# Placing the next norm's steps of both pairs between the products of the second channel matmul

## The chip, the cores and the metric

The kernel runs on one core of one Trainium2 chip. The metric is the device time of one execution in microseconds (us), as the median of several runs. Engines are named as the profile names them: PE (TensorE, matmuls), PEld (its weight loads), DVE (VectorE), ACT (ScalarE), POOL (GpSimd), SP (SyncE, which issues most DMAs here). Each engine works through its own instructions strictly in order; an instruction can wait for semaphores of other engines and of DMAs.

## The reference, cut to what matters

Three layers run one after the other on 8 x 576 = 4608 rows of 512 columns: attention with pooled keys and values, a mixture of experts, and a channel mix with a norm before it. The change lies in the last:

```python
mu = np.mean(x, axis=-1, keepdims=True)
var = np.mean((x - mu) ** 2, axis=-1, keepdims=True)
xn = (x - mu) / np.sqrt(var + 1e-06) * g_ln
ch = np.maximum(xn @ w_ch1, 0.0) @ w_ch2      # 512 -> 2048 -> 512
return (x + ch).astype(np.float32)
```

## The kernel before, in words

The attention and the experts take the first half of the time (up to about 660 us) and are not touched. After them the channel mix goes through the 4608 rows in `NG` = 9 passes of 512 rows (g = 0 to 8). A pass is `ffn1(g)` and then `ffn2(g)`: the first and the second channel matmul.

Both matmuls are computed with seven products of blocks in place of eight (`PROD`, numbered 1 to 7), and each product in fp16 with three matmuls, high half x high half, high x low and low x high (`PASS`). A product of the second matmul is one call of `mm2(i, pr)`: 8 slices x 3 = 24 matmuls of 128x256. The index i is the pair: pair 0 holds the row tiles 4g and 4g+2, pair 1 the tiles 4g+1 and 4g+3 (a tile is 128 rows). Products 1, 6, 5 and 3 of a pair accumulate one after the other in the PSUM tile `ga[i]`, products 2, 7 and 4 in `gb[i]`. Between two products the result so far must be read out of PSUM: `ev2(g, i, pr)` does it, by an ACT copy for products 1 and 6 (L1075) and 7 (L1077), by DVE for 2 (L1079), 5 (L1082), 4 (L1085) and 3. So product 6 of pair 0 can't start before ACT's copy of product 1 of pair 0, product 7 not before L1079 of the same pair, product 5 not before the copy of product 6, product 4 not before the copy of product 7. PE takes the products of `ffn2` in this order: 1 and 2 of pair 0 and 1 of pair 1 (their last slice at the end), then (1,2), (0,6), (0,7), (1,6), (1,7), (0,5), (1,5), (0,4), (1,4), written as (pair, product). Product 3 is left over and runs inside the next `ffn1`.

Meanwhile the rows of the next pass have to be normed and transposed. `ln(g, i, q)` does this for one pair. It is a Python generator of 21 steps, each of which issues one piece:

- steps 1 to 8: the statistics of both tiles on DVE (L995 to L998, L1001, L1002), with two small POOL operations (L999);
- steps 9 to 11: three ACT operations that write the normed rows into q (L1004, L1006 twice);
- steps 12 to 15: four DVE sums and differences of blocks (`combine`, L862);
- step 16: an ACT copy that rounds seven blocks to fp16, the high half `q16[:, 0]` (L1008);
- step 17: a DVE subtraction that writes the low half `q16[:, 1]` (L1009);
- steps 18 to 21: four DMA transposes issued by SP (L1014), from `q16` into `xnT`. Taken as 28 blocks of 128 columns, the transposes carry blocks 0 to 7, 8 to 15, 16 to 23 and 24 to 27. Blocks 0 to 13 are the high half, 14 to 27 the low half, two for each of the seven inputs.

There is one `q16` and one `xnT` for both pairs; q is `q32[0]` for pair 0 and `q32[1]` for pair 1 (the traces call them q and r). Every matmul of `ffn1` reads the columns of both pairs. A product of `ffn1` (`mm1`, six matmuls) takes the high half of its input in the first two matmuls and the low half in the third. Its first three products are 1, 2 and 6: they need low blocks 14 and 15 (second transpose), 16 and 17 (third) and 24 and 25 (fourth).

What sets the order is the order in which the Python code issues instructions, for each engine on its own. `tick(n)` takes n steps from a list of generators, `chains`: pair 0 first, and pair 1 once pair 0 is through. `drain()` takes all that is left.

Of the kernel before, what the change touches and what calls it, by code (L numbers as in the profile page):

```python
# [9 lines left out]
F32 = mybir.dt.float32  # L10
# [38 lines left out]
def tile_attention_moe_ffn(ctx: ExitStack, tc: tile.TileContext, a, out):  # L49
# [71 lines left out]
    with ExitStack() as at:  # L121
# [257 lines left out]
        for i in range(NT + 3):  # L379
# [49 lines left out]
            if i < NT and b + 2 < B:  # L429
                g = f - 2 if b == 0 else f  # L430
# [30 lines left out]
    def single(name, *shape, dt=F32):  # L461
        return ctx.enter_context(tc.tile_pool(name=f"{name}_p", bufs=1)).tile([128, *shape], dt, name=name)
# [5 lines left out]
    q32 = [single("q32", 8, 256), r2[:, 0:2048].rearrange("p (b x) -> p b x", x=256)]  # L468
# [37 lines left out]
    chains = []  # L506

    def tick(n=1):
        while chains and n:
            if next(chains[0], None) is None:  # L510
                chains.pop(0)
            else:
                n -= 1
# [97 lines left out]
    m2 = ctx.enter_context(tc.tile_pool(name="m2", bufs=2))  # L611
    ps_m = ctx.enter_context(tc.tile_pool(name="ps_m", bufs=2, space=PSUM))
    with ExitStack() as rt:
# [3 lines left out]
        def sb(name, *shape, dt=F32):  # L617
            return rp.tile([128, *shape], dt, name=name)
# [11 lines left out]
        st = sb("st", 2, 128)  # L630
# [225 lines left out]
    def combine(q, rows):  # L856
        if rows:
            ops = ((4, 0, 3, ADD), (5, 1, 0, SUB), (6, 1, 4, SUB), (7, 2, 6, ADD))
        else:
            ops = ((4, 0, 1, SUB), (5, 3, 0, SUB), (6, 4, 3, SUB), (7, 2, 6, ADD))  # L860
        for o, x, y, f in ops:
            yield V.tensor_tensor(out=q[:, o], in0=q[:, x], in1=q[:, y], op=f)  # L862
# [122 lines left out]
    def ln(g, i, q):  # L985
        st_t = []
        for j in (4 * g + i, 4 * g + 2 + i):
            yt = yt_t[j]
            ti = ym.tile([128, 1], U32, tag="ti", name="ti")
            ti_t[j] = ti  # L990
            st = m2.tile([128, 6], F32, tag="bs", name="bs")
            mv = m2.tile([128, 2], F32, tag="mv", name="mv")
            rs = m2.tile([128, 2], F32, tag="rs", name="rs")
            st_t.append((yt, mv, rs))
            yield V.bn_stats(out=st, in_=yt[:, 0:DM])  # L995
            yield V.bn_aggr(out=mv, in_=st)
            V.tensor_copy(out=ti, in_=yt[:, DM:YROW])
            V.tensor_scalar(out=rs[:, 0:1], in0=mv[:, 1:2], scalar1=1e-6, scalar2=None, op0=ADD)  # L998
            yield P.tensor_tensor(out=rs[:, 0:1], in0=rs[:, 0:1], in1=mhalf, op=ALU.pow)  # L999
        for yt, mv, rs in st_t:  # L1000
            V.tensor_scalar(out=rs[:, 0:1], in0=rs[:, 0:1], scalar1=SN, scalar2=None, op0=ALU.mult)  # L1001
            yield V.tensor_scalar(out=rs[:, 1:2], in0=mv[:, 0:1], scalar1=rs[:, 0:1], scalar2=-1.0, op0=ALU.mult, op1=ALU.mult)  # L1002
        (x, _, rx), (y, _, ry) = st_t
        yield A.activation(out=q[:, 1:3], in_=x[:, 0:DM].rearrange("p (b x) -> p b x", x=256), func=AF.Identity, scale=rx[:, 0:1], bias=rx[:, 1:2])  # L1004
        for h in range(2):
            yield A.activation(out=q[:, 3 * h], in_=y[:, 256 * h:256 * h + 256], func=AF.Identity, scale=ry[:, 0:1], bias=ry[:, 1:2])  # L1006
        yield from combine(q, False)
        yield A.copy(out=q16[:, 0], in_=q[:, 1:8])  # L1008
        yield V.tensor_tensor(out=q16[:, 1], in0=q[:, 1:8], in1=q16[:, 0], op=SUB)  # L1009
        dst = xnT.rearrange("p x m c t -> p (x m c) t")  # L1010
        src = q16.rearrange("p x m c -> p (x m c)")
        for n in range(0, 28, 8):
            w = min(8, 28 - n)
            yield nc.sync.dma_start_transpose(out=dst[:, n:n + w, 128 * i:128 * i + 128], in_=src[:, 128 * n:128 * n + 128 * w])  # L1014

    def drain():
        while chains:
            tick()


    NG = NT // 4
# [22 lines left out]
    def mm2(i, pr, lo=0, hi=NP):  # L1044
        m, n = PROD[pr]
        if pr == 1 and lo == 0:
            ga[i] = ps_m.tile([128, 512], F32, tag="m", name="ga")
        if pr == 2 and lo == 0:
            gb[i] = ps_y.tile([128, 512], F32, tag="y", name="gb")
        ps = (ga if pr in (1, 6, 5, 3) else gb)[i]  # L1050
        for p in range(lo, hi):
            for x, w in PASS:
                nc.tensor.matmul(  # L1053
                    out=ps[:, 0:256], lhsT=hw[:, p, x, m, 128 * i:128 * i + 128], rhs=c2w[:, p, w, n],
                    start=(pr in (1, 2, 7) and p == 0 and x + w == 0), stop=(p == NP - 1 and x == 1), skip_group_check=True,
                )

    def out_rows(j):
        P.indirect_dma_start(  # L1059
            out=out, out_offset=bass.IndirectOffsetOnAxis(ap=ti_t.pop(j), axis=0),  # L1060
            in_=yt_t.pop(j)[:, 0:DM], in_offset=None,
        )

    def ev2(g, i, pr):
        u, t, v = us[3 * i:3 * i + 3]
        X, Y = yt_t.get(4 * g + i), yt_t.get(4 * g + 2 + i)
        lo, hi = slice(0, 256), slice(256, 512)
        a2 = ga[i][:, 0:256]
        b2 = gb[i][:, 0:256] if pr != 1 else None

        def add(row, c, src):
            V.scalar_tensor_tensor(out=row[:, c], in0=src, scalar=SC, in1=row[:, c], op0=ALU.mult, op1=ADD)  # L1072

        if pr in (1, 6):
            A.copy(out=v if pr == 1 else u, in_=a2)  # L1075
        elif pr == 7:
            A.copy(out=t, in_=b2)  # L1077
        elif pr == 2:
            V.tensor_tensor(out=v, in0=b2, in1=v, op=ADD)  # L1079
            add(X, lo, v)  # L1080
        elif pr == 5:
            V.tensor_tensor(out=t, in0=a2, in1=t, op=ADD)  # L1082
            add(Y, hi, t)
        elif pr == 4:
            V.tensor_tensor(out=u, in0=b2, in1=u, op=ADD)  # L1085
            add(Y, lo, u)
            out_rows(4 * g + 2 + i)
        elif pr == 3:
            add(X, hi, a2)
            out_rows(4 * g + i)  # L1090
# [67 lines left out]

    def ffn2(g):
        L = NP - 1  # L1160
        tick(8)
        mm2(0, 2, 0, L)
        tick(7)
        mm2(1, 1, 0, L)
        for i, pr in ((0, 1), (0, 2), (1, 1)):
            mm2(i, pr, L)
            ev2(g, i, pr)
        tick(6)
        for i, pr, n in ((1, 2, 0), (0, 6, 8), (0, 7, 7), (1, 6, 0), (1, 7, 6), (0, 5, 0), (1, 5, 0), (0, 4, 0), (1, 4, 0)):
            mm2(i, pr)  # L1170
            ev2(g, i, pr)
            tick(n)
        drain()


    def ahead(k):
# [14 lines left out]
    for k in range(NF + 2):  # L1191
# [51 lines left out]
        if k in (NF - 5, NF - 2):  # L1243
            chains.append(ln(0, int(k > NF - 5), q32[0]))
# [3 lines left out]
    drain()  # L1248
    for g in range(NG):
        ffn1(g)  # L1250
        if g + 1 < NG:
            chains.extend(ln(g + 1, i, q32[i]) for i in range(2))
        ffn2(g)
    for i in range(2):
        mm2(i, 3)
# [58 lines left out]
```

## Time and profile before

| | |
|---|---|
| median of 3 runs | 1337.65 us (1333.14 to 1343.53) |
| profiled execution | 1343.89 us, of which the span from first to last instruction is 1342.1 us |
| mean granted TensorE clock | 0.984 |
| busy share of the span | PE 95%, PEld 70%, DVE 67%, ACT 47%, POOL 23% |
| one pass of the channel mix | 74.40 us (from the start of product (0,6) at 709.64 us to the same at 784.04 us) |

The profile is of one execution. Its times are in us from the first instruction. In the timeline each row is an instruction, or a run of equal ones, with start, duration, engine, line, what it writes and reads, and in brackets how long the engine had been idle before it and who ended that.

### The profile page before, as it was taken

What the parts mean: (1) busy time and instruction counts of PE and PEld (TensorE: products, weight loads), DVE (VectorE), ACT (ScalarE), POOL (GpSimd) and SP (SyncE); (2) the same over time, 40 slices, a digit from 0 to 9 for tenths busy, and PEclk for the clock granted to TensorE, in tenths of its full rate; (3) what the DMA queues carried; (4) which work ended last, traced back from release to release, by engine and by line L of the source; (5) the groups of instructions that cost most, each with busy time, mean ns of one, the idle gap of its engine ahead of it and who ended that gap; (6) DMA issues with size and microseconds to landing.
All of it is one profiled execution on the core that took longest, in us unless ns stands there. A gap on an engine that the chain in (4) does not pass through costs nothing. (4 is left out here: it accounts for less than half of the span.)

```text
span 1342.1 us, 26386 instructions
## 1 busy us (share of the span) xinstructions
PE 1280.8 (95%) x9232; PEld 938.2 (70%) x9232; DVE 898.4 (67%) x2029; ACT 624.7 (47%) x1279; POOL 302.7 (23%) x315
## 2 busy tenths in 40 slices
PE   5999988999989999998899999999999999999996
PEld 4888854444444444443488888888888888888885
DVE  6666778545565656657595867768686868778671
ACT  4667633333544535455453635444353535444340
POOL 3455513242424243331101010101000010101001
PEclk8999989999999999998899999999999999999998
DMA  8877245999999989889963645455454645554410
GB/s 265 266 245 242 88 166 146 248 200 201 226 227 196 239 170 204 210 227 255 272 223 73 213 110 185 126 156 168 120 208 99 206 98 204 119 181 139 128 70 32
DMA packets 229101, 239.94 MB, mean 179 GB/s; under 512 B 160846, under 2 KB 179534, under 8 KB 228944
## 3 DMA queue, kind: packets, MB, share of 16 engines
q1 hardware_dynamic: 190560, 154.96, 44.5%
q10 hardware_dynamic: 29184, 53.48, 14.2%
q0 software_dynamic: 9200, 29.57, 7.2%
q8 instruction: 77, 1.26, 0.4%
q14 instruction: 80, 0.66, 0.2%
HBM read 282.61 MB, written 36.62 MB: 238 GB/s over the span
## 5 line engine op out<-in xcount | busy, mean ns | idle before, releaser
L1053 PEld LDWEIGHTS <-w 128*128 128x128 f16 x3024 | 295.8, 98 | 41.9 <-issue 7.7
L583 PE MATMUL h_ps<-w,r 128*128 128x512 f16 x936 | 217.0, 381 | 12.8 <-ACTq L961 4.5
L596 PE MATMUL y_ps<-w,hTb 128*128 128x512 f16 x936 | 219.6, 385 | 8.6 <-DMA hTb<-r 4.1
L1053 PE MATMUL ga<-c2w,w 128*128 128x256 f16 x1728 | 208.1, 273 | 6.3 <-ACT hTb L1075 6.3
L596 PEld LDWEIGHTS <-hTb 128*128 128x128 f16 x936 | 92.5, 99 | 124.2 <-issue 9.6
L583 PEld LDWEIGHTS <-r 128*128 128x128 f16 x936 | 91.8, 98 | 117.6 <-issue 17.4
L1053 PE MATMUL gb<-c2w,w 128*128 128x256 f16 x1296 | 150.3, 273 | 0.0
L1059 POOL DMA_INDIRECT out_dram<-ytb,ti x26 | 29.6, 1137 | 371.7 <-DVE ytb L1072 342.1
L1039 PEld LDWEIGHTS <-ld 128*128 128x128 f16 x1008 | 98.5, 98 | 12.9 <-issue 1.0
L1039 PEld LDWEIGHTS <-r 128*128 128x128 f16 x1008 | 98.6, 98 | 12.4 <-issue 0.6
L1039 PEld LDWEIGHTS <-w 128*128 128x128 f16 x1008 | 98.6, 98 | 12.2 <-issue 0.3
L588 DVE SCALAR_TENSOR_TENSOR r<-h_ps,r 128x512 f16<-128x512 f32 x59 | 40.5, 687 | 80.0 <-ACT r L587 39.1
L604 POOL DMA_INDIRECT y_d<-ytb,sidx x39 | 41.5, 1064 | 209.9 <-ACT r L548 136.4
L522 DVE SCALAR_TENSOR_TENSOR w<-w 128x1024 f16<-128x1024 f32 x55 | 65.5, 1232 | 23.7 <-ACT w L517 21.2
L1039 PE MATMUL fa<-xnT,ld 128*128 128x256 f16 x576 | 78.6, 273 | 0.1
L1039 PE MATMUL fa<-xnT,r 128*128 128x256 f16 x576 | 78.6, 273 | 0.1
L1039 PE MATMUL fa<-xnT,w 128*128 128x256 f16 x576 | 78.6, 273 | 0.0
L517 ACT ACTIVATE w<-w 128x1024 f16<-128x1024 f32 x56 | 55.7, 1047 | 31.4 <-ACTq L963 11.1
L587 ACT ACTIVATE r<-h_ps 128x512 f16<-128x512 f32 x59 | 35.1, 594 | 74.0 <-PE h_ps L583 44.8
L268 ACT ACTIVATE p<-s,nm 128x72 f32<-128x72 f32 x288 | 65.6, 337 | 4.2 <-DVE nm L254 4.0
L1097 ACT COPY hTb<-fa 128x256 f32<-128x256 f32 x72 | 26.8, 372 | 85.7 <-PE fa L1039 85.7
L549 DVE SCALAR_TENSOR_TENSOR r<-x_ps,r 128x512 f16<-128x512 f32 x39 | 26.9, 689 | 49.7 <-ACT r L548 47.5
(247 smaller groups left out, 2121.2 us busy)
## 6 DMA issues: line engine op xcount, KB each, us to landing
w<-in_w_dram ACTq DMA_DIRECT2D x136, 1024.0 KB
ld<-c_d SPq DMA_DIRECT2D x24, 896.0 KB
w<-c_d SPq DMA_DIRECT2D x24, 896.0 KB
r<-c_d SPq DMA_DIRECT2D x24, 896.0 KB
ld<-in_c_dram ACTq DMA_DIRECT2D x48, 256.0 KB
xrow_d<-xr SPq DMA_DIRECT2D x36, 260.5 KB
kt<-in_kT_dram SPq DMA_DIRECT2D x16, 576.0 KB
qt<-in_qT_dram SPq DMA_DIRECT2D x18, 512.0 KB
```

Source lines behind the costliest of these rows:

```text
L268: nc.scalar.activation(out=p32[:, h, :], in_=s[:, h // 4, NK * (h % 4):NK * (h % 4) + NK], func=AF.Exp, bias=nm[:, h:h + 1],)
L517: A.activation(out=hi, in_=src, func=AF.Copy, scale=SW)
L522: V.scalar_tensor_tensor(out=lo[:, 0:v], in0=src[:, 0:v], scalar=SW, in1=hi[:, 0:v], op0=ALU.mult, op1=ALU.subtract)
L549: V.scalar_tensor_tensor(out=xT[:, 1], in0=pt, scalar=SX, in1=xT[:, 0], op0=ALU.mult, op1=ALU.subtract)
L583: nc.tensor.matmul(out=ps, lhsT=xT[:, x, c], rhs=s1[:, w, c, 512 * half:512 * half + 512], start=(n == 0), stop=(n == 11))
L587: A.activation(out=hs[:, 0], in_=ps, func=AF.Relu)
L588: V.scalar_tensor_tensor(out=hs[:, 1], in0=ps, scalar=0.0, in1=hs[:, 0], op0=ALU.max, op1=ALU.subtract)
L596: nc.tensor.matmul(out=ps, lhsT=hT[:, f // 4, x, f % 4], rhs=s2[:, w, f], start=(f == 0 and x + w == 0), stop=(f == 7 and x == 1),)
L604: nc.gpsimd.indirect_dma_start(out=y_d[:, :], out_offset=bass.IndirectOffsetOnAxis(ap=sidx[:, k:k + 1], axis=0), in_=yr, in_offset=None, b ...
L1039: nc.tensor.matmul(out=ps[:, 0:256], lhsT=w[:, x, m, 128 * c:128 * c + 128], rhs=xnT[:, y, n, c], start=(pr in (1, 2, 7) and i + c == 0), ...
L1053: nc.tensor.matmul(out=ps[:, 0:256], lhsT=hw[:, p, x, m, 128 * i:128 * i + 128], rhs=c2w[:, p, w, n], start=(pr in (1, 2, 7) and p == 0 an ...
L1059: P.indirect_dma_start(out=out, out_offset=bass.IndirectOffsetOnAxis(ap=ti_t.pop(j), axis=0), in_=yt_t.pop(j)[:, 0:DM], in_offset=None,)
```

## The change

The list `chains` is no longer used by `ffn2`. It makes one generator for each pair and takes the steps of either by `step(i, n)`; `full(i, pr)` is a product and its read-out. The order of the products on PE stays, and so do all instructions: only the places of the norm's steps between the read-outs change, and both norms are under way at once. Because of that the small tiles of the statistics get four buffers in place of two. The last pass has no next norm.

```diff
@@ ln
-            st = m2.tile([128, 6], F32, tag="bs", name="bs")
-            mv = m2.tile([128, 2], F32, tag="mv", name="mv")
-            rs = m2.tile([128, 2], F32, tag="rs", name="rs")
+            st = m2.tile([128, 6], F32, tag="bs", name="bs", bufs=4)
+            mv = m2.tile([128, 2], F32, tag="mv", name="mv", bufs=4)
+            rs = m2.tile([128, 2], F32, tag="rs", name="rs", bufs=4)
@@ ffn2
         L = NP - 1
-        tick(8)
+        norm = [ln(g + 1, i, q32[i]) if g + 1 < NG else iter(()) for i in range(2)]
+
+        def step(i, n):
+            for _ in range(n):
+                next(norm[i], None)
+
+        def full(i, pr):
+            mm2(i, pr)
+            ev2(g, i, pr)
+
+        step(0, 8)
         mm2(0, 2, 0, L)
-        tick(7)
         mm2(1, 1, 0, L)
         for i, pr in ((0, 1), (0, 2), (1, 1)):
             mm2(i, pr, L)
             ev2(g, i, pr)
-        tick(6)
-        for i, pr, n in ((1, 2, 0), (0, 6, 8), (0, 7, 7), (1, 6, 0), (1, 7, 6), (0, 5, 0), (1, 5, 0), (0, 4, 0), (1, 4, 0)):
-            mm2(i, pr)
-            ev2(g, i, pr)
-            tick(n)
-        drain()
+        step(0, 3)
+        step(1, 8)
+        full(1, 2)
+        step(0, 5)
+        full(0, 6)
+        step(0, 5)
+        step(1, 3)
+        full(0, 7)
+        step(1, 4)
+        full(1, 6)
+        step(1, 1)
+        full(1, 7)
+        step(1, 5)
+        for i, pr in ((0, 5), (1, 5), (0, 4), (1, 4)):
+            full(i, pr)
@@ the passes
         ffn1(g)
-        if g + 1 < NG:
-            chains.extend(ln(g + 1, i, q32[i]) for i in range(2))
         ffn2(g)
```

On ACT, in one pass, from the end of `ffn1` to the end of `ffn2`, before (q_2208 and r_2200 are q of pair 0 and of pair 1, q_2212 is `q16`, hTb holds the buffers that the copies from PSUM write):

```order
L1004 ACTIVATE q_2208<-hTb,rs 128x512
L1006 ACTIVATE q_2208<-ytb,rs 128x256 x2
L1075 COPY hTb<-ga 128x256 x2
L1008 CAST q_2212<-q_2208 128x1792
L1075 COPY hTb<-ga 128x256
L1077 COPY hTb<-gb 128x256
L1004 ACTIVATE r_2200<-hTb,rs 128x512
L1006 ACTIVATE r_2200<-ytb,rs 128x256 x2
L1075 COPY hTb<-ga 128x256
L1077 COPY hTb<-gb 128x256
L1008 CAST q_2212<-r_2200 128x1792
```

And the same stretch of ACT with the change:

```order
L1075 COPY hTb<-ga 128x256 x2
L1004 ACTIVATE q_2208<-hTb,rs 128x512
L1006 ACTIVATE q_2208<-ytb,rs 128x256 x2
L1008 CAST q_2212<-q_2208 128x1792
L1075 COPY hTb<-ga 128x256
L1004 ACTIVATE r_2200<-hTb,rs 128x512
L1006 ACTIVATE r_2200<-ytb,rs 128x256 x2
L1077 COPY hTb<-gb 128x256
L1075 COPY hTb<-ga 128x256
L1008 CAST q_2212<-r_2200 128x1792
L1077 COPY hTb<-gb 128x256
```

The copies of product 1 of both pairs now stand ahead of pair 0's norm; pair 1's norm stands ahead of the copies of (0,7) and (1,6), and pair 1's L1008 ahead of the copy of (1,7).

On DVE, behind the statistics of pair 0 (their last row stands first), before:

```order
L1002 TENSOR_SCALAR rs<-mv,rs 128x1
L862 TENSOR_TENSOR q_2208<-q_2208 128x256 x4
L1079 TENSOR_TENSOR hTb<-gb,hTb 128x256
L1072 SCALAR_TENSOR_TENSOR ytb<-hTb,ytb 128x256
L1009 TENSOR_TENSOR q_2212<-q_2208,q_2212 128x1792
L1079 TENSOR_TENSOR hTb<-gb,hTb 128x256
L1072 SCALAR_TENSOR_TENSOR ytb<-hTb,ytb 128x256
L995 BN_STATS bs<-hTb 128x6
```

With the change the twelve rows of pair 1's statistics follow on the first read-out (L1079, L1072) at once, and after their last row DVE goes on with:

```order
L1002 TENSOR_SCALAR rs<-mv,rs 128x1
L1079 TENSOR_TENSOR hTb<-gb,hTb 128x256
L1072 SCALAR_TENSOR_TENSOR ytb<-hTb,ytb 128x256
L862 TENSOR_TENSOR q_2208<-q_2208 128x256 x4
L1009 TENSOR_TENSOR q_2212<-q_2208,q_2212 128x1792
L862 TENSOR_TENSOR r_2200<-r_2200 128x256 x4
L1009 TENSOR_TENSOR q_2212<-r_2200,q_2212 128x1792
L1082 TENSOR_TENSOR hTb<-ga,hTb 128x256
```

Pair 0's L862 and L1009 moved behind pair 1's statistics and behind both read-outs L1079. The two L1009, which both write `q16`, have only pair 1's four L862 between them.

## Rows read from the trace of the kernel before

All rows are of one pass, 1060 to 1110 us, where nothing else is said.

**Rows 1.** Busy time by stretch: engines, then granted clock, DMA share, GB/s.
```profile
core 0: us, PE busy (x) PEld busy (x) DVE busy (x) ACT busy (x) POOL busy (x), PEclk, DMA share, GB/s
1077.00:1082.00 5.00, 4.21 (x40) 3.63 (x38) 3.71 (x16) 2.39 (x5) 1.11 (x2) 1.00 0.09 37
1082.00:1102.00 20.00, 20.00 (x186) 17.92 (x184) 12.79 (x30) 6.65 (x9) 1.74 (x3) 1.00 0.56 93
```

**Rows 2.** What L1053 waited for over the whole run: us, times.
```profile
  issue: 7.7, 8
  ACT hTb L1075: 6.3, 8
```

**Rows 3.** Timeline, PE: products (1,2), (0,6), (0,7), and the next `ffn1`.
```profile
1078.07 2.78 PE L1053 MATMUL gb<-c2w,w 128*128 128x256 f16 x24
...
1081.64 2.78 PE L1053 MATMUL ga<-c2w,w 128*128 128x256 f16 x24 [0.79 <-ACT hTb L1075]
...
1084.26 2.78 PE L1053 MATMUL gb<-c2w,w 128*128 128x256 f16 x24
...
1102.60 0.82 PE L1039 MATMUL fa<-xnT,ld 128*128 128x256 f16 x6
```

**Rows 4.** Timeline, ACT: pair 0's norm, copies of product 1, both L1008.
```profile
1079.48 0.81 ACT L1004 ACTIVATE q<-ytb,rs 128x512 f32<-128x512 f32 x1 [3.67 <-DVE rs L1002]
...
1080.25 1.09 ACT L1006 ACTIVATE q<-ytb,rs 128x256 f32<-128x256 f32 x2
...
1081.24 0.62 ACT L1075 COPY hTb<-ga 128x256 f32<-128x256 f32 x2
...
1082.67 1.69 ACT L1008 CAST q<-q 128x1792 f16<-128x1792 f32 x1 [0.80 <-ACT hTb L1075]
...
1092.81 1.69 ACT L1008 CAST q<-r 128x1792 f16<-128x1792 f32 x1
```

**Rows 5.** Timeline, DVE: the rows of both norms and one read-out.
```profile
1080.00 0.21 DVE L1002 TENSOR_SCALAR rs<-mv,rs 128x1 f32<-128x1 f32 x1
...
1080.88 1.71 DVE L862 TENSOR_TENSOR q<-q 128x256 f32<-128x256 f32 x4 [0.67 <-ACT q L1006]
...
1082.51 0.42 DVE L1079 TENSOR_TENSOR hTb<-gb,hTb 128x256 f32<-128x256 f32 x1
...
1082.96 0.42 DVE L1072 SCALAR_TENSOR_TENSOR hTb<-hTb 128x256 f32<-128x256 f32 x1
...
1084.38 2.03 DVE L1009 TENSOR_TENSOR q<-q,q 128x1792 f16<-128x1792 f32 x1 [1.00 <-ACT q L1008]
...
1087.12 0.69 DVE L995 BATCH_NORM_STATS2 bs<-ytb 128x6 f32<-128x512 f32 x1
...
1090.13 0.21 DVE L1002 TENSOR_SCALAR rs<-mv,rs 128x1 f32<-128x1 f32 x1
...
1094.52 2.02 DVE L1009 TENSOR_TENSOR q<-r,q 128x1792 f16<-128x1792 f32 x1 [1.80 <-ACT q L1008]
```

**Rows 6.** SP's queue: the issue of pair 1's second transpose.
```profile
1096.58 1.23 SPq L1014 DMA_TRANSPOSE xnT<-q  x1
```

**Rows 7.** DMA rate in slices of 0.05 us, 1096 to 1098 and 1100 to 1102.
```profile
GB/s 205 230 205 225 205 220 225 189 215 215 195 195 225 200 225 174 148 241 196 124 62 26 0 0 0 0 0 0 0 0 0 0 0 0 0 67 148 189 225 205
...
GB/s 230 189 205 236 169 159 226 185 108 62 72 123 174 205 200 220 205 200 246 205 210 215 159 103 57 37 16 0 0 0 0 0 0 0 0 0 0 0 0 0
```

**Rows 8.** DMA rate, 259.5 to 261.5, and PE's wait for a transpose there.
```profile
GB/s 108 67 92 87 67 92 61 102 72 82 26 77 61 51 87 200 15 26 215 271 307 271 307 292 282 302 262 253 276 297 297 282 302 271 302 276 302 276 307 271
...
260.73 0.39 PEld L596 LDWEIGHTS <-hTb 128*128 128x128 f16 x3 [3.57 <-DMA hTb<-ytb]
```

**Rows 9.** DMA rate from 1336 us to the end of the span (slices of 0.15 us).
```profile
GB/s 376 430 349 242 0 0 0 0 0 0 0 0 0 0 0 0 0 0 0 0 0 0 376 430 376 376 161 0 0 0 0 0 0 0 0 0 0 0 0 0
```

**Rows 10.** DMA, pair 0's transposes: queues 1088 to 1090, busy tenths 1090 to 1092.
```profile
q8 instruction: 1, 0.02, 2.9%
...
DMA  0000010100001000001003999999999999999999
```

**Rows 11.** Timeline, POOL: output rows behind product (0,4).
```profile
1101.35 1.03 POOL L1059 DMA_INDIRECT out_dram<-ytb,ti  x1 [11.45 <-DVE ytb L1072]
```

## The prediction

> **What bounds the kernel now.** I read the busy time by stretch first. In the channel mix PE is the bound: from 1082 to 1102 it is busy 20.00 of 20.00 us at a granted clock of 1.00, while ACT and DVE have room [rows 1]. So only what makes PE wait counts. Next I asked what the line of the second matmul waits for: all over the run one thing, ACT's copy L1075, eight times, once in each pass that has a next pass [rows 2]. The timeline of PE shows the place: product (1,2) starts at 1078.07, (0,6) at 1081.64, 3.57 us later, where the next one follows after 2.62 [rows 3]. So a pass loses 0.95 us. (The row itself says 0.79, because the ends of matmuls are modelled; the weight loads' wait, 7.7 us over eight, agrees with 0.95.)
>
> The timeline of ACT says why. Product (0,1) was through before (1,2) began, but its copy starts only at 1081.24: it stands behind L1004 and L1006 of the next norm, and L1004 had itself waited 3.67 us for the statistics [rows 4]. It is a queue problem, not a lack of time.
>
> **What the change takes away.** The two copies of product 1 stand ahead of L1004, on an ACT that is idle until 1079.48 [rows 4]. PE needs the first one at 1080.69 (1078.07 + 2.62). So the 0.95 us should go in each of the eight passes: 7.6 us. Nothing is added to any engine, and what PE executes is the same. If nothing else came late, that would be all.
>
> **What comes late instead.** In the rest I write 81.64 for 1081.64. The statistics of pair 0 end at 80.21. DVE then does a read-out (L1079 and L1072, 0.90 us by their pitch), the statistics of pair 1 (87.12 to 90.34, so 3.22), another read-out (0.90) and only then pair 0's L862 (1.71): until 86.97, where before it ended at 82.59 [rows 5]. ACT follows 0.08 later with L1008 (1.69) [rows 4], then L1009 (2.03): it ends at 90.80, before at 86.41. Pair 0's low half is 4.4 us later.
>
> *Read-outs on ACT.* The copy of (0,6) stands behind this L1008 and runs at about 88.9 to 89.2; (0,5) needs it at 91.17. Then L1004 and L1006 of pair 1 (0.77 + 1.09), the copies of (0,7) and (1,6) until 91.8; (1,5) needs the latter at 93.79. Both keep 2.0 us. The copy of (1,7) is behind pair 1's L1008, done below at 95.5, and needed at 99.03. These cost nothing; their cover is two whole products.
>
> *Read-outs on DVE.* L1082 of (0,5), ready at 93.95, will stand behind pair 1's L1009 until 98. Its PSUM tile is next written by product 3 in the following `ffn1`, about 2.6 us after that begins. No cost.
>
> *The transposes.* Here the cover is thin. Pair 1's second transpose is issued at 96.58 [rows 6], 0.04 us after its L1009 ends; packets flow from 97.70, and the last ones of the fourth transpose end at 101.3 [rows 7]. So four transposes need 4.75 us from the end of L1009, and the second of them 2.6 (1.12 until the packets flow, then 3.6 us for two and a half transposes, 1.44 each). What passes between the last packet and an engine that waits for it this pass doesn't show, because nothing waited. The nearest row is PE's wait for a transpose in the experts' part: the packet rate falls to 15 and 26 GB/s at 260.30 to 260.40, and the weight load starts at 260.73 [rows 8]: 0.4 us. The lower bound is 0. The upper bound is the end of the kernel, where the last packets end at 1340.1 and the span at 1342.1: 2.0 us, for a store to DRAM with all that ends a program [rows 9]. I take 0.4, since it is the same kind of transfer.
>
> The Trainium skill (DMA: Bandwidth & Descriptors, section Anatomy of one DMA) speaks against the change here: it gives a DMA a fixed cost of about 2.0 us, most of it the write receipt after the last byte. That is written for DMAs issued by GpSimd; less the 1.12 us ahead of the packets it would leave 0.9, and the sum below would be a loss of about 5 us in place of a gain of 3. The row with 0.4 decides for me.
>
> Now the chain, which passes through that end twice. `q16` is one buffer. Pair 1's L1008 may overwrite its high half when pair 0's first two transposes have read it, its L1009 the low half after all four. L862 of pair 1 would be done at 92.5, so before the transposes are: L1008 starts at 90.80 + 2.6 + 0.4 = 93.8 and ends at 95.5. L1009 starts at 90.80 + 4.75 + 0.4 = 95.95 and ends at 97.97; before it ended at 96.54. The fourth transpose of pair 1 is usable at 97.97 + 5.15 = 103.12. PE would begin `ffn1` at 101.65 (102.60 - 0.95 [rows 3]); its third product needs that transpose 14 matmuls of 0.109 us later, less 0.1 for the weight load, at 103.08. That is 0.04 late, which is nothing, but the reserve, which before was 2.3 us, is gone. The second and third transposes come earlier against their need.
>
> What then decides are hiccups. In this pass the transposes of pair 0 stopped from 1090.0 to 1091.05, about when an instruction fetch (q8) shows [rows 10]; they ended at 92.05, not at 86.41 + 4.75: 0.9 late. It cost nothing, having cover. I found such a pause in five of the six passes looked at, in four of them at a place that would now count. So 4/6 x 0.9 = 0.6 us a pass is given back.
>
> **Sum.** 8 x (0.95 - 0.6) = 2.8 us less. The profiled execution took 1343.89 us, 6.2 more than the median of the runs shown. 1343.9 - 2.8 = 1341.1 there; against the median, 1337.65 - 2.8, about **1335 us**. Chance 0.42.
>
> **Rivals.**
>
> 1. *The full gain.* The transposes land in time in every pass: the chain is some 0.5 us shorter than I reckon, or pauses fall into the 1.2 us in which pair 1's first transpose waits for nothing. For it: my lateness without pauses is only 0.04. Against it: four of six. 1336.3 in the profile's terms, 1330 against the median. Chance 0.25.
>
> 2. *Slower: PE waits for the transposes at the start of each `ffn1`, for longer than it waited for the copy.* It needs the end of a transpose to take longer than 0.4 us, and counts that twice. The balance tips at 0.4 + 0.35 / 2 = 0.58 us. At 0.9, between the bounds, a pass loses 0.6 + 1.0 - 0.95 = 0.65 us, 5.2 in all: 1342.9 against the median; at the upper bound of 2.0, 2.85 a pass, 23 in all: 1360. (0.9 is also what the figure of the Trainium skill, DMA: Bandwidth & Descriptors, leaves; see above.) For it: everything is now in one chain, and POOL's output rows, issued at 1101.35 [rows 11], move 0.95 us forward with PE, onto pair 1's last transpose. Against it: the 0.4 us. Chance 0.25.
>
> 3. *The copy isn't what PE waits for.* Then (0,6) still starts 0.95 late, and the time stays at 1338. Against it: the next row of PE comes 0.4 us after L1075 begins, eight times over. Chance 0.08.
>
> **Range and chances.** The lower end is the full gain with the scatter of a median of three (the runs shown lie 4.5 us below to 5.9 above theirs): 1328. The upper end takes in rival 2 up to an end of about 1.1 us: 1346. A measurement of this kernel tells about 1%, 13 us, from no change. The most that the change can gain is 7.6, so faster by over 1% is left to scatter, 0.03. Slower by over 1% needs an end of 1.4 us or more: 0.07. Within 1%: 0.90.
>
> **What the profile after would show.** PE's row for (0,6) has no wait for L1075 and starts 2.62 us after (1,2). ACT's L1008 of pair 1 is ended in its wait by a DMA, starting near 93.8 on this pass's scale; L1009 of pair 1 waits for a DMA too. If PE waits anew, it is at L1039 for xnT, in the first three products of `ffn1`, and unevenly over the passes. The forecast is wrong if that wait is absent in all passes (rival 1) or over 0.95 us in most (rival 2); and if PE waits for L1075 or L1077 later in the pass, my reading of the ACT queue is.

## The result, and the profile after

The changed kernel took 1350.06 us (median of nine runs, 1343.42 to 1354.54), the kernel before 1339.78 us (nine runs, 1333.14 to 1344.52): ratio 1.008, 95% interval 1.0057 to 1.0104. That is some 10 us slower, where 2.8 us faster was forecast. The profiled execution of after took 1343.42 us (span 1341.7), the lowest of its nine. Its channel mix begins at 653.84 us, before's at 659.84, so spans don't compare. The channel mix alone does: a pass with nothing in its way takes 73.45 us, and from one start of (0,6) to the next I count what a pass has above that. Before loses 0.95 in each of eight passes, 7.6 us in all (the first of them ahead of the first start that is counted). After it is 12.85 us: periods of 74.65, 74.44, 75.16, 75.67, 74.60, 75.32, 74.97 and 75.64. Net: 5.25 us lost.

All that PE waited for after 700 us (line, releaser, us in all, times, longest), in after:

```profile
PE fa L1039 <- DMA xnT<-q: 8.2, 10, 1.8
PE fb L1039 <- DMA xnT<-q: 2.5, 5, 0.8
```

In before the same list had one row, L1053 for the copy L1075, eight times [rows 2]. That wait is gone; its line now shows no idle time. In its place stand fifteen waits for transposes in the first products of `ffn1`. The timeline of PE shows one pass, the one that [rows 3] show of before:

```profile
1074.66 2.78 PE L1053 MATMUL gb<-c2w,w 128*128 128x256 f16 x24
1077.28 2.78 PE L1053 MATMUL ga<-c2w,w 128*128 128x256 f16 x24
...
1098.24 0.82 PE L1039 MATMUL fa<-xnT,ld 128*128 128x256 f16 x6
1098.89 0.82 PE L1039 MATMUL fb<-xnT,ld 128*128 128x256 f16 x6
1099.55 0.38 PE L1039 MATMUL fa<-xnT,ld 128*128 128x256 f16 x2
1101.72 0.61 PE L1039 MATMUL fa<-xnT,ld 128*128 128x256 f16 x4 [1.79 <-DMA xnT<-q]
```

(0,6) follows (1,2) after 2.62 us, as forecast. Then the third product of `ffn1` stops after two of its six matmuls, the two that need the high half, and waits for the fourth transpose.

The same pass on ACT, to be read against [rows 4]; subtract 3.41 us from a time of before or of the forecast to get one on this scale:

```profile
1074.26 0.37 ACT L1075 COPY hTb<-ga 128x256 f32<-128x256 f32 x1 [1.86 <-PE ga L1053]
1074.86 0.37 ACT L1075 COPY hTb<-ga 128x256 f32<-128x256 f32 x1 [0.23 <-PE ga L1053]
1076.07 0.82 ACT L1004 ACTIVATE q<-ytb,rs 128x512 f32<-128x512 f32 x1 [0.83 <-DVE rs L1002]
...
1083.07 1.69 ACT L1008 CAST q<-q 128x1792 f16<-128x1792 f32 x1 [5.14 <-issue]
...
1090.16 1.69 ACT L1008 CAST q<-r 128x1792 f16<-128x1792 f32 x1 [2.91 <-DMA xnT<-q]
```

And on DVE, against [rows 5]:

```profile
1077.51 0.69 DVE L995 BATCH_NORM_STATS2 bs<-ytb 128x6 f32<-128x512 f32 x1
...
1080.53 0.21 DVE L1002 TENSOR_SCALAR rs<-mv,rs 128x1 f32<-128x1 f32 x1
...
1081.45 1.54 DVE L862 TENSOR_TENSOR q<-q 128x256 f32<-128x256 f32 x4
1084.79 2.02 DVE L1009 TENSOR_TENSOR q<-q,q 128x1792 f16<-128x1792 f32 x1 [1.79 <-ACT q L1008]
...
1092.24 2.02 DVE L1009 TENSOR_TENSOR q<-r,q 128x1792 f16<-128x1792 f32 x1 [3.96 <-ACT hTb L1077]
```

Here the chain that was forecast can be checked off. Pair 1's statistics stand ahead of pair 0's L862. Pair 1's L1008 waits for pair 0's transposes, since there is one `q16`, and starts at 1090.16 (forecast 1090.39 on this scale). L1009 is put down to ACT's L1077, but its operands were ready at 1091.85, when L1008 ended. It started at 1092.24 (forecast 1092.54), 0.64 us behind the last packets of pair 0's transposes, for which it must wait too. It ended at 1094.26, and the fourth transpose should have been usable 5.15 us later, at 1099.4. PE got it at 1101.72. So the miss lies behind L1009. POOL's store of output rows, against [rows 11], shows what else was going on there:

```profile
1096.99 1.03 POOL L1059 DMA_INDIRECT out_dram<-ytb,ti  x1 [16.68 <-DVE ytb L1072]
```

Next the DMA queues of after, in two stretches behind that end of L1009: 1098.86 to 1099.86, then 1099.86 to 1101.26. The columns are packets, MB and share of the 16 DMA engines; q1 carries SP's transposes, q0 POOL's stores.

```profile
q0 software_dynamic: 73, 0.25, 63.1%
q1 hardware_dynamic: 109, 0.02, 10.8%
q8 instruction: 1, 0.02, 7.4%
...
q0 software_dynamic: 7, 0.02, 4.6%
q1 hardware_dynamic: 3, 0.00, 0.1%
```

At the moment when the transposes should have ended (1099.01), the stores' packets start, on the same 16 engines. The last 0.02 MB of the transposes are drawn out among them, the very last packet past 1101. The row of q8 is a fetch of instructions: 7.4% of 16 engines for 1 us, so 1.18 us of one engine, in the same stretch. So the 1.79 us of this pass are not the stores' alone; the experiments below tell the two apart. In before the stores' packets began 6.4 us behind the end of L1009, when the transposes were over.

### The profile page after: what moved, and what is told of

It reads as the page before. It is cut to its first block, busy times and chain, and to the rows that moved or that the text cites. A ratio compares the mean times of both kernels' runs of the same rounds, so it can differ in the third digit from the quotient of the medians.

```text
span 1341.7 us, 26385 instructions
## 1 busy us (share of the span) xinstructions
PE 1280.0 (95%) x9232; PEld 936.9 (70%) x9232; DVE 895.7 (67%) x2029; ACT 622.7 (46%) x1279; POOL 301.0 (22%) x315
## 5 line engine op out<-in xcount | busy, mean ns | idle before, releaser
L1053 PEld LDWEIGHTS <-w 128*128 128x128 f16 x3024 | 295.9, 98 | 34.2
L1053 PE MATMUL ga<-c2w,w 128*128 128x256 f16 x1728 | 208.1, 273 | 0.0
L1053 PE MATMUL gb<-c2w,w 128*128 128x256 f16 x1296 | 150.3, 273 | 0.0
L1059 POOL DMA_INDIRECT out_dram<-ytb,ti x26 | 26.4, 1014 | 424.6 <-DVE ytb L1072 391.1
L1039 PE MATMUL fb<-xnT,w 128*128 128x256 f16 x432 | 59.4, 273 | 1.2 <-DMA xnT<-q 1.2
```

Of the source, the lines that this page charges most:

```text
L1039: nc.tensor.matmul(out=ps[:, 0:256], lhsT=w[:, x, m, 128 * c:128 * c + 128], rhs=xnT[:, y, n, c], start=(pr in (1, 2, 7) and i + c == 0), ...
L1053: nc.tensor.matmul(out=ps[:, 0:256], lhsT=hw[:, p, x, m, 128 * i:128 * i + 128], rhs=c2w[:, p, w, n], start=(pr in (1, 2, 7) and p == 0 an ...
L1059: P.indirect_dma_start(out=out, out_offset=bass.IndirectOffsetOnAxis(ap=ti_t.pop(j), axis=0), in_=yt_t.pop(j)[:, 0:DM], in_offset=None,)
```

## The experiments

Seven kernels ran. Each answers to one step; the periods are those of its profiled execution. A ratio, with its 95% interval, is an estimate from all runs of both kernels and not the quotient of the two medians.

**The copy alone.** The kernel before with only its copies of product 1 put ahead of pair 0's L1004; both norms still one after the other.

```diff
         mm2(0, 2, 0, L)
-        tick(7)
         mm2(1, 1, 0, L)
...
-        tick(6)
+        tick(13)
```

> The kernel before with one part of the change alone: the copies of product 1 go ahead of the next norm's ACT steps (steps 9 to 21 of pair 0 are issued behind the three read-outs, all else as before). Theory (the change lost because pair 0's transposes came 4 us later, pair 1's norm had to wait for them, and pair 1's transposes then ended too late for ffn1): here pair 0's rows stay where they were, so pair 1's transposes end when they did, PE's 0.95 us in each of eight passes go and nothing comes back: 5 to 7.6 us less than before, ratio 0.994 to 0.9965, no or little wait of L1039 for xnT (under 2 us in all). Rival 1 (it is the output rows' stores, which move 0.95 us forward with PE and fall onto the last transposes): they move forward here just the same, so PE waits for the transposes in most passes, 0.5 to 1.5 us each, and the time is that of before or slower, ratio 0.998 to 1.005. Rival 2 (the loss is not in the channel mix): as before, 1.000, or slower.

Ratio 0.9964 (0.9933 to 0.9996), median 1336.97 against 1340.35. All eight periods are 73.45 us. ACT in one pass:

```profile
1069.17 0.37 ACT L1075 COPY hTb<-ga 128x256 f32<-128x256 f32 x1 [1.86 <-PE ga L1053]
1069.77 0.37 ACT L1075 COPY hTb<-ga 128x256 f32<-128x256 f32 x1 [0.23 <-PE ga L1053]
1070.98 0.81 ACT L1004 ACTIVATE q<-ytb,rs 128x512 f32<-128x512 f32 x1 [0.83 <-DVE rs L1002]
```

So the first step holds: by the periods the 7.6 us are all there to be had by the place of the copies, and PE waits for nothing else. The runs by themselves say less: the interval allows a gain of 0.5 to 9 us.

**The stores later.** The kernel after, with the rows of product 4 stored behind the first slice of `ffn1`. A small POOL copy of an operand that is written there holds the stores back.

```diff
-            out_rows(4 * g + 2 + i)
+            late.append(4 * g + 2 + i)
...
+            if s == 0:
+                out_late(q32[0][:, 3, 0:1])
```

> The changed kernel, but POOL stores the output rows of products (0,4) and (1,4) only after the fifth product of the following ffn1 (a one-column POOL copy that reads the result of L1152 stands ahead of them). Theory (late transposes alone): PE's waits for xnT stay at about 12.9 us over the eight passes, ratio to the kernel before 1.004 to 1.008. Rival 1 (the stores hold up the last transposes' completion): the waits for the fourth transpose shrink from 1 to 2 us a pass to 0 to 1, the sum of the losses falls to 3 to 7 us, ratio 0.997 to 1.001. Rival 2 (not in the channel mix): 1.008 as with the change.

Ratio 0.9998 (0.9966 to 1.0029): level with before. Periods 74.30, 73.59, 74.05, 74.95, 74.42, 74.59, 73.82, 75.06: 7.18 us lost, where after lost 12.85. By these two profiles the stores cost the difference, 5.7 us. That is the first rival of the expectation (3 to 7 us left, ratio up to 1.001), a little above its sum. PE's waits for transposes here (all lines are one later in this kernel):

```profile
PE fb L1040 <- DMA xnT<-q: 3.0, 6, 0.6
PE fa L1040 <- DMA xnT<-q: 2.4, 3, 1.1
```

By transpose, from the single rows of the timelines: in after the fourth was waited for 8 times (7.0 us), the third 5 times (2.5), the second twice (1.2); here the fourth once (1.06 us), the third 6 times (3.0), the second twice (1.3). The stores hit the fourth transpose alone, the one that is still under way when they start. A pass that nothing else disturbs shows it best: the queues from 1024.93 to 1025.93 in after, 4.6 to 5.6 us behind the end of L1009,

```profile
q0 software_dynamic: 78, 0.25, 66.0%
q1 hardware_dynamic: 99, 0.02, 9.6%
```

and the same stretch of the same pass here (1025.51 to 1026.51):

```profile
q1 hardware_dynamic: 84, 0.01, 7.5%
```

When the last packet of the transposes came, in us behind the end of pair 1's L1009 (end of the slice of 0.2 us that holds it, from the queues):

| pass | 1 | 2 | 3 | 4 | 5 | 6 | 7 | 8 |
|---|---|---|---|---|---|---|---|---|
| before | 5.0 | 5.2 | 6.0 | 4.8 | 5.0 | 5.0 | 6.0 | 5.0 |
| stores later | 4.8 | 5.2 | 5.8 | 5.0 | 5.0 | 5.8 | 5.6 | 5.0 |
| after | 5.8 | 6.2 | 7.0 | 5.6 | 5.4 | 7.0 | 6.8 | 5.6 |

In after the stores' first packets come 4.5 to 4.9 us behind L1009 in every pass, and the last of the transposes 0.4 to 1.2 us later than without them. The Trainium skill (DMA: Bandwidth & Descriptors, section Queues, rings and completion order) says that each DMA engine takes turns between the queues that have work for it, packet by packet. The mixed packets of q0 and q1 agree with that; here q0's hold 0.25 MB in 78, q1's 0.02 MB in 99. That a small packet which takes its turn behind a large one gives up much is argued from these sizes; no run varied them.

The periods show one thing more. In the second pass of this run no packet of q8 falls among the transposes, from pair 0's second to pair 1's fourth, and 0.14 us are lost. In each of the other seven one does, with 0.9 to 1.6 us of one DMA engine, and these passes lose 0.37 to 1.61 us, 7.04 in all. In after the second pass loses 0.99 and the other seven 1.15 to 2.22. So in the one pass without such a fetch the change is about level (0.99 lost for 0.95 won), and the net loss comes from the seven others.

**The buffers alone.** The kernel before with four buffers for the statistics, nothing else.

```diff
-            st = m2.tile([128, 6], F32, tag="bs", name="bs")
+            st = m2.tile([128, 6], F32, tag="bs", name="bs", bufs=4)
```

(and `mv`, `rs` likewise)

> The kernel before with only the four buffers in place of two for the statistics' small tiles; the order of all instructions stays. Theory and rival 1: no change, ratio 0.998 to 1.002, PE still waits 8 times for L1075. Rival 2 (memory layout or anything else that is not the order): slower, 1.003 to 1.008.

Ratio 0.9997 (0.9965 to 1.0029), and the row of before comes back:

```profile
PE ga L1053 <- ACT hTb L1075: 6.3, 8, 0.8
```

So the four buffers, and the layout in memory that they bring, are no part of it.

**The copy alone, with the stores later.** Both edits above, on the kernel before.

> Both parts: the copies first as in the first kernel and the stores late as in the second. Theory (late transposes alone): like the first kernel, 5 to 7.6 us less than before, ratio 0.994 to 0.9965. Rival 1 (the stores): also 5 to 7.6 us less, while the first kernel is not faster than before. Rival 2: as before.

Ratio 0.9969 (0.994 to 0.9998), median 1334.86 against 1340.35, all periods 73.45. Against the copy alone nothing is gained: moving the stores is worth something only where transposes are late.

**The change again, twice.** The same kernel, to see how far its loss is the same from run to run; no edit.

> The changed kernel once more, to see how its losses scatter. In the first profile PE lost 12.9 us to late transposes over eight passes and won back 7.6, 5.3 in all, while the runs show 10.7 us more than before. Theory (the losses depend on where instruction fetches and stores fall, and differ from run to run): another profile shows another sum, up to 18 us, and ratio 1.005 to 1.010. Rival (something outside the channel mix adds 5 us): the sum is again 12 to 13.5 us, with the same ratio.

Ratio 1.0046 (1.001 to 1.0082). 13.92 us lost in the periods, so 6.3 net: a sum just above the rival's, with a ratio just below the theory's range. PE's waits:

```profile
PE fa L1039 <- DMA xnT<-q: 8.4, 10, 1.9
...
PE fb L1039 <- DMA xnT<-q: 3.5, 6, 1.0
```

> The changed kernel a third time, as the run above: theory, a sum of PE's losses in the channel mix that differs from the first two by over 1 us; rival, the same 12 to 13.5 us.

Ratio 1.0015 (0.998 to 1.0051), which alone is not told from no change. 16.3 us lost in its periods (over 1 us from the first two, as the theory had it), 8.7 net, though 1.7 of that are a matter of the clock (last section). The three profiles put the loss in the channel mix at 5.3, 6.3 and 8.7 us. The three ratios scatter more than that, and the first and third intervals just miss each other. The part ahead of the channel mix is the same code everywhere and ended between 652.9 and 667.4 us over the nine profiles. A scatter of that size in single executions may be the reason; this isn't shown, and what moves that part stays open.

**Pair 1's statistics later.** The kernel after with one line moved. On DVE pair 0's L862 and L1009 now stand ahead of pair 1's statistics; the two norms no longer overlap there.

```diff
         step(0, 3)
-        step(1, 8)
         full(1, 2)
         step(0, 5)
         full(0, 6)
         step(0, 5)
+        step(1, 8)
         step(1, 3)
```

> The changed kernel with one line moved: the eight statistics steps of pair 1 come after pair 0's norm is through (behind its transposes), no longer ahead of product (1,2). Theory (on DVE these 3.2 us ahead of pair 0's L862, with the read-out of (1,2) behind them, make all transposes late): pair 0's L1009 ends about 3 us sooner, pair 1's norm waits for no transpose, PE waits for xnT under 1 us in all, the eight times 0.95 us are won: ratio 0.994 to 0.9975. Rival (the change loses by other placements: pair 1's ACT steps ahead of the copies of (0,7) and (1,6), the stores): the waits for xnT or for an ACT copy stay over 5 us in all, ratio 1.000 to 1.008.

Ratio 0.9948 (0.992 to 0.9975), median 1332.99 against 1341.95: it beats the kernel before and, by the intervals, the changed one. All periods are 73.44 to 73.46 us. One pass, ACT and DVE, the rows that waited for transposes in after:

```profile
1095.66 1.69 ACT L1008 CAST q<-r 128x1792 f16<-128x1792 f32 x1 [0.81 <-ACT hTb L1075]
```

```profile
1088.04 2.03 DVE L1009 TENSOR_TENSOR q<-q,q 128x1792 f16<-128x1792 f32 x1 [1.79 <-ACT q L1008]
1089.98 0.69 DVE L995 BATCH_NORM_STATS2 bs<-ytb 128x6 f32<-128x512 f32 x1
...
1097.38 2.03 DVE L1009 TENSOR_TENSOR q<-r,q 128x1792 f16<-128x1792 f32 x1 [1.80 <-ACT q L1008]
```

and PE:

```profile
1083.62 2.78 PE L1053 MATMUL ga<-c2w,w 128*128 128x256 f16 x24
...
1104.58 0.82 PE L1039 MATMUL fa<-xnT,ld 128*128 128x256 f16 x6
1105.24 0.82 PE L1039 MATMUL fb<-xnT,ld 128*128 128x256 f16 x6
1105.89 0.82 PE L1039 MATMUL fa<-xnT,ld 128*128 128x256 f16 x6
```

From (0,6) to L1009 of pair 0 it is 4.42 us in place of 7.51, 3.1 less, about the 3.22 of the statistics. From (0,6) to pair 1's L1009 it is 13.76 in place of 14.96. So 1.2 us of chain decide the sign: L1009 ends 5.17 us ahead of `ffn1`, in after 3.98. The stores begin 5.2 to 5.7 us behind L1009, mostly past the end of the transposes. The reserve is not large: in the third pass, after a pause and with the stores among them, the last packets of q1 came 6.4 us behind L1009. PE did not wait there either.

## Why the prediction was wrong

- *What bounds the kernel, and the gain of 7.6 us*: right. In the periods the copy alone and the last kernel give back exactly the eight times 0.95 us.
- *The read-outs on ACT and DVE at no cost*: right. PE waits nowhere for L1075, L1077 or L1082 in after, and L1008 of pair 1 is ended in its wait by a DMA eight times (25.2 us in all).
- *The chain through DVE and `q16`*: right to 0.3 us as far as pair 1's L1009, in the pass that was worked out, but with luck. Pair 0's L1009 ended at 1086.81, 0.58 sooner than reckoned (90.80 is 1087.39 on this scale), and from there to the start of pair 1's L1009 it took 5.43 us in place of 5.15; the two errors offset each other in part. (Two slips beside that are small: the terms named for pair 0's L862 add up to 86.94, not 86.97, and the packets of [rows 7] run from 97.75 to 101.35, so four transposes need 4.80 us.)
- *The transposes' lateness without the stores*: mis-sized. The forecast gave 0.6 us a pass for pauses and 0.04 for the chain, 4.8 in all; with the stores out of the way 7.18 us were lost. The pass of that run without a fetch among the transposes lost 0.14: eight times that is 1.1 us, against 0.3 for the chain (an estimate from a single pass). The other 6 us stand in the seven passes with a fetch, where the forecast had 4.8: it counted a pause in four passes of six. In the chain itself two things were off. The end of a transpose took longer than the 0.4 us of [rows 8]: pair 0's fourth transpose had its last packets at 791.78 in one pass and 1091.60 in the other, and L1009 started at 792.33 and 1092.24, 0.55 and 0.64 later; its second reaches L1008 after 0.7 to 0.8. These lie about or beyond the 0.58 at which the forecast saw its balance tip; yet the pass without a fetch lost only 0.14, with pair 0's L1009 sooner than reckoned. And "the second and third transposes come earlier against their need" is wrong: with the stores late, eight of nine waits are for them.
- *The stores*: this is the step that failed. They were named under the second rival, "move 0.95 us forward with PE, onto pair 1's last transpose", and then priced at nothing, in the sum and in the rival. They cost 5.7 us against the profile of after (6.7 and 9.1 against the other two of the changed kernel). The trace of before would have given the overlap: there the stores' packets began 6.4 us behind L1009's end, at 1102.94. Moved 0.95 forward that is 1101.99, while the same forecast had the transposes run to 97.97 + 4.75, on that scale 1102.72.
- *The signs together*: forecast 4.8 - 7.6 = -2.8; measured 7.18 + 5.7 - 7.6 = +5.3 in the profiled channel mix. The second rival is what happened, with its place and its sign. An end of 0.9 to 2.0 us, from which it had its price, was the smaller part at most: from a last packet of a transpose to the engine that waited for it the trace of after has 0.5 to 0.9 us, and 1.2 to 1.3 for L1009 in two passes with a fetch at that place.
- *The root* is one placement, and the forecast had it too, as its 4.4 us: pair 1's statistics ahead of pair 0's L862. Taking just that back, with all else of the change in place, removes both losses.

Left open: what the single `q16` costs by itself, since no run had a second one; and what the fetches cost, which stand in the traces at the pauses but which no run moved.

## What to carry to other kernels

When an edit moves a chain later and the bound engine earlier, lay the transfers of every queue on one time scale on both sides of the edit, those that nobody waits for as well: a store that is harmless on its own delays the transfer that is awaited if their packets meet. If the reserve of a step comes out as nothing, its unknown terms decide the sign and each needs a price, however small. Where two chains share one buffer, as `q16` here, overlapping their beginnings on a common engine delays the first one, and the second waits for it anyway.

## What the runs showed of the hardware that was not expected

*The clock fell after a wait of 2.08 us.* In one pass of the third run of the change PE waited 2.08 us for the fourth transpose. PE's timeline there:

```profile
807.80 0.61 PE L1039 MATMUL fa<-xnT,w 128*128 128x256 f16 x4 [2.08 <-DMA xnT<-q]
808.25 1.09 PE L1039 MATMUL fb<-xnT,w 128*128 128x256 f16 x6
809.13 1.49 PE L1053 MATMUL ga<-c2w,w 128*128 128x256 f16 x6
810.41 1.49 PE L1039 MATMUL fa<-xnT,w 128*128 128x256 f16 x6
```

and its busy time by stretch (columns as in [rows 1]):

```profile
810.00:812.00 2.00, 2.00 (x11) 1.44 (x10) 0.00 (x0) 0.00 (x0) 0.00 (x0) 0.50 0.13 51
812.00:814.00 2.00, 2.00 (x20) 1.76 (x19) 0.85 (x2) 0.37 (x1) 0.00 (x0) 0.98 0.00 0
```

From 810 to 812 the granted clock was 0.50, the lower level (1.2 GHz), and six matmuls took 1.49 in place of 0.82 us. That pass had a period of 77.45 us, some 1.7 more than its waits explain; the clock of 0.66 from 808 to 810, 0.50 and then 0.98 gives up just that (0.68, 1.00 and 0.04 us). After the waits of 1.79 us in after and 1.89 us in the second run of the change the granted clock stayed at 1.00. The fall was seen once; that the wait brought it about was not tested.

*Fetches of instructions stand where transposes pause.* With the stores later, in the sixth pass a packet of q8 came at about 1099.0, within 0.1 us of where the transposes should have ended; after it their packets stopped, and the last five came after 1099.9. PE waited for those 1.06 us, the only wait for a fourth transpose in that run. [Rows 10] show the like in before. The same run has a fetch among the transposes in every pass but the second, and only that one loses as little as 0.14 us. That the fetch is the cause is read from where it stands in time only; no run moved it.
